# Fused windowed attention and MLP on one core: the early pairs, the weight decoding and the first shared slices put in one written order, with double weight chunks

## The chip, the cores and the metric

One core of a Trainium2 chip runs the whole program. The metric is the device time of one execution in microseconds (us). The kernel before took 674.14 us as the median of three runs (673.58 to 674.37). The engines are TensorE (PE in the profile; PEld is its weight load), VectorE (DVE), ScalarE (ACT), GpSimd (POOL) and SyncE (SP), whose queue issues nearly all DMAs.

## The reference, cut to what matters

```python
# attention: B=4, H=8, S=768, D=64, fp32
scores = scale * q @ k.T                      # per head
keep   = (column < 8) | (0 <= row - column < 96)
scores = where(keep, scores - slope[h] * dist, -1e9)
a = exp(scores - max(scores));  a = a / (sum(a) + 1e-9)
x = (a @ v) laid out as [B*S, H*D] = [3072, 512]
# MLP: w_in [512, 2048], w_out [2048, 512]
h = x @ w_in
g = h * clip(h + 3, 0, 6) / 6
out = g @ w_out                               # [3072, 512]
```

The two weight matrices reach the kernel as 64-bit floats (two 32-bit words for each value) and are turned into 32-bit values on the chip; this is the decoding below. Each 32-bit value is then split in a high and a low part of type fp32r, so that three fp32r products stand for one exact one.

## The kernel before, in words

**Tiling.** The 3072 rows are eight blocks of 384 rows (three tiles of 128). A block's attention is four pairs of heads; 32 pairs in all, numbered n = 0 to 31. The MLP of a block has 16 slices of 128 hidden columns. A slice is a first product (`first`, L165: 12 matmuls of 384 columns into a bank hp), a gate (`gate`: ACT at L182, DVE at L183), a split of the gated values into high and low (`high`: ACT at L191 in the first two blocks, POOL at L189 later; `rest`: DVE at L196) and a second product (`second`, L199: 9 matmuls of 512 columns into three acc banks). TensorE runs `second` of a slice only after `first` of the next slice.

**A pair.** `scores` (matmuls, L818), `weigh` (six DVE sums with a running minimum at L833, six ACT exponentials at L837), `sum_up` (DVE, L847 and L848), `normalize` (six POOL multiplications, L857), `turn` (transposes on TensorE at L865 and L867, copied out to pt at L869), `values` (matmuls, L909) and `put_x` (ACT at L157, DVE at L158).

**The early part** (`banded`, L488). Pairs 0 to 11 (`EARLY` = 12) fill x of the first three blocks. A loop over n scores pair n + 2, normalizes pair n + 1, turns pair n and multiplies pair n - 1 by the values, so four pairs are in work at once. From n = 8 on, halves of the first MLP slices of block 0 are put in between; `FIRST` = 6 such slices run here. After the loop the remaining slices of blocks 0 and 1 alternate ("shared slices": both blocks use the same decoded weights). Blocks 2 to 7 follow, each with the attention of the next block between its slices.

**Decoding** (`decode`, L393). There are 32 chunks of 128x512 values. For one chunk: a DMA (L368); ACT takes the absolute value of the upper word (wz, L376); POOL scales the lower word (we, L380); DVE clamps (L407) and shifts left by three (L408); ACT makes the sign from the upper half word (L387); DVE adds the two (L417); ACT rounds to the high part (w1h or w2h, L421); DVE subtracts for the low part (w1l or w2l, L414). The loads have three buffers (`WORDS`), wz and we two each. `work(pe, dve)` keeps an account of TensorE and DVE time and emits a decoding step when DVE is behind; `decoded_to` forces the steps that a slice needs.

**Order.** TensorE, SP and POOL execute in the order in which the program text emits their instructions (`in_order`, L615, a chain of order-only dependencies). ACT and DVE are ordered by the scheduler from its own estimate of times. `load_next` (L297) issues the load of a later pair behind the matmuls that free its buffer.

Of the kernel before, what the change touches and what calls it, by code (L numbers as in the profile page):

```python
# [9 lines left out]
F32 = mybir.dt.float32  # L10
# [3 lines left out]
I16 = mybir.dt.int16  # L14
F16 = mybir.dt.float16
# [6 lines left out]
P = 128  # L22
NT = 3
# [23 lines left out]
BOTH = 10  # L47
ROOMS = 2
MORE = 3
LEAD = 6  # L50
WAKE = 9
FIRST = 6
WORDS = 3
DOWN = 2.0 ** -95
# [8 lines left out]
class Kernel:  # L63
# [15 lines left out]
    def decoding(self, ctx, loads, bufs, **kw):  # L79

        self.wp = self.pool("wp", loads, ctx=ctx, **kw)
        self.zp = self.pool("zp", bufs, ctx=ctx, **kw)
        self.ep = self.pool("ep", bufs, ctx=ctx, **kw)
# [16 lines left out]
    def constants(self):  # L100
# [4 lines left out]
        self.small = self.const.tile([P, 4], F32, name="small")  # L105
        self.three, self.half = self.small[:, 0:1], self.small[:, 3:4]
        nc.vector.memset(self.three, 3.0)
        nc.vector.memset(self.half, -0.5)
# [8 lines left out]
    def weight_chunk(self, i):  # L117
# [17 lines left out]
        nc.sync.dma_start(out=st, in_=self.w[i])  # L135
# [18 lines left out]
    def put_x(self, x, pair, ps):  # L154
        nc = self.nc
        xh, xl = x
        nc.scalar.copy(out=xh[:, pair, :], in_=ps)  # L157
        nc.vector.tensor_tensor(out=xl[:, pair, :], in0=ps, in1=xh[:, pair, :].bitcast(F32), op=ALU.subtract)  # L158
# [74 lines left out]
    def bank(self, what):  # L233

        s, t, x, o, h = ((self.ps_s, "sp"), (self.ps_t, "tp"), (self.ps_x, "xp"), (self.ps_o, "acc"), (self.ps_h, "hp"))
        pools = {"s": (s, o, o, o), "t": (t, h, h), "x": (x,)}[what] if self.more else {"s": (s, t)[:self.score_banks], "t": (t,), "x": (x,)}[what]
# [129 lines left out]
    def fetch(self, i):  # L366
        self.raw[i] = self.wp.tile([P, 2 * DM], I32, name="wst")
        self.nc.sync.dma_start(out=self.raw[i], in_=self.w[i])  # L368

    def magnitude(self, i):  # L370
# [3 lines left out]
        self.z[i] = self.zp.tile([P, DM], I32, name="wz")  # L374
        self.e[i] = self.ep.tile([P, DM], I32, name="we")
        self.nc.scalar.activation(out=self.z[i].bitcast(F32), in_=words[:, :, 1].bitcast(F32), func=AF.Abs, scale=DOWN)  # L376
        if i == 0:
            self.tc.add_manual_dep(self.nc.cur_bb.bb.instructions[-1], self.held, mybir.DependencyInfo(
                mybir.DependencyClass.NoSync, mybir.DependencyReason.DATA), reason="behind the first pairs")
        self.nc.gpsimd.tensor_scalar(out=self.e[i], in0=words[:, :, 0].bitcast(U32), scalar1=2.0 ** -29, scalar2=0.0, op0=ALU.mult, op1=ALU.add)  # L380

    def signs(self, i):


        top = self.raw[i].bitcast(I16).rearrange("p (c w) -> p c w", w=4)[:, :, 3]
        over = self.e[i].bitcast(F16).rearrange("p (c w) -> p c w", w=2)[:, :, 1]
        self.nc.scalar.activation(out=over, in_=top, func=AF.Sign, scale=-1.0, bias=self.half)  # L387

    def part(self, i, w1, w2):
        f = i // 2  # L390
# [598 lines left out]
```

## Time and profile before

| what | value |
|---|---|
| median of three runs | 674.14 us (673.58 to 674.37) |
| the profiled execution, device time | 675.05 us |
| its span, first to last instruction | 673.2 us |
| busy TensorE, VectorE, ScalarE, GpSimd | 655.6, 406.0, 299.2, 216.1 us |
| mean granted TensorE clock | 0.996 |

The profile is of one execution; what lies around its span is 675.05 - 673.2 = 1.85 us. A busy TensorE is not one at its peak, since ends of matmuls are modelled and matmuls that fill a pause (the kernel's `spin`) count as busy. In rows that list instructions in order of time, the first column is the start and the second the duration; the difference of two starts is what an instruction costs its engine, since the durations of neighbours overlap by about 0.1 us.

### The profile page before, as it was taken

What the parts mean: (1) busy time and instruction counts of PE and PEld (TensorE: products, weight loads), DVE (VectorE), ACT (ScalarE), POOL (GpSimd) and SP (SyncE); (2) the same over time, 40 slices, a digit from 0 to 9 for tenths busy, and PEclk for the clock granted to TensorE, in tenths of its full rate; (3) what the DMA queues carried; (4) which work ended last, traced back from release to release, by engine and by line L of the source; (5) the groups of instructions that cost most, each with busy time, mean ns of one, the idle gap of its engine ahead of it and who ended that gap; (6) DMA issues with size and microseconds to landing.
All of it is one profiled execution on the core that took longest, in us unless ns stands there. A gap on an engine that the chain in (4) does not pass through costs nothing.

```text
span 673.2 us, 11394 instructions
## 1 busy us (share of the span) xinstructions
PE 655.6 (97%) x3963; PEld 586.4 (87%) x3963; DVE 406.0 (60%) x1090; ACT 299.2 (44%) x768; POOL 216.1 (32%) x389
## 2 busy tenths in 40 slices
PE   9888799999999999999999999999999999999996
PEld 7767688889999999899998999899998999989995
DVE  6788789982224776457663777447763677422222
ACT  6899899962225433144332443143331434231111
POOL 5655722210001343234341454314431444302110
PEclk9989999999999999999999999999999999999999
DMA  8678565500003267525644267624555255510001
GB/s 294 180 217 273 174 206 195 188 32 0 1 1 133 69 173 201 153 81 140 178 120 132 87 171 184 173 96 117 141 166 141 78 149 141 142 48 2 0 1 52
DMA packets 60835, 84.72 MB, mean 126 GB/s; under 512 B 8416, under 2 KB 45536, under 8 KB 60768
## 3 DMA queue, kind: packets, MB, share of 16 engines
q1 hardware_dynamic: 60480, 83.64, 42.6%
q8 instruction: 33, 0.54, 0.3%
q14 instruction: 34, 0.28, 0.1%
q10 hardware_dynamic: 288, 0.26, 0.1%
HBM read 62.92 MB, written 20.97 MB: 125 GB/s over the span
## 4 chain that ended last, share of the span: by engine, by line
PE 89%; DMA 3%; DVE 2%; POOL 2%; ACT 2%; issue 1%; SPq 0%; POOLq 0%; DVEq 0%
PE hp L171 38%; PE acc L203 33%; PE xp L909 4%; PE sp L822 2%; DMA wst<-w 2%; PE tp L909 2%; PE sp L203 2%; PE tp L203 2%; PE xp L203 2%; PE tp L822 2%; POOL n L857 1%; PE sp L818 1%; ACT n L837 1%; POOL we L380 1%; ACT we L387 1%
## 5 line engine op out<-in xcount | busy, mean ns | idle before, releaser
L182 ACT ACTIVATE g<-hp,small 128x384 f32<-128x384 f32 x127 | 73.7, 580 | 261.6 <-PE hp L171 234.2
L171 PE MATMUL hp<-xh,w1h 128*128 128x384 f32 x512 | 174.0, 340 | 0.0
L171 PE MATMUL hp<-xh,w1l 128*128 128x384 f32 x512 | 172.7, 337 | 0.0
L171 PE MATMUL hp<-xl,w1h 128*128 128x384 f32 x512 | 171.9, 336 | 0.0
L189 POOL TENSOR_SCALAR gh<-g 128x384 fp32r<-128x384 f32 x96 | 51.8, 540 | 292.7 <-DVE g L183 253.9
L203 PE MATMUL acc<-w2h,gl 128*128 128x512 f32 x336 | 133.1, 396 | 0.0
L203 PE MATMUL acc<-w2l,gh 128*128 128x512 f32 x336 | 132.4, 394 | 0.0
L203 PE MATMUL acc<-w2h,gh 128*128 128x512 f32 x336 | 132.1, 393 | 0.0
L183 DVE SCALAR_TENSOR_TENSOR g<-g,hp 128x384 f32<-128x384 f32 x128 | 69.7, 545 | 101.5 <-ACT g L182 101.3
L857 POOL TENSOR_SCALAR n<-n,sums 128x232 f32<-128x232 f32 (+1 forms) x186 | 101.4, 561 | 36.9 <-DVE sums L848 24.8
L196 DVE TENSOR_TENSOR gl<-g,gh 128x384 fp32r<-128x384 f32 x128 | 79.2, 619 | 53.6 <-POOL gh L189 45.5
L837 ACT ACTIVATE n<-n,least 128x232 f32<-128x232 f32 (+1 forms) x192 | 89.3, 467 | 43.1 <-DVE least L833 42.1
L171 PEld LDWEIGHTS hp<-xh,w1h 128*128 128x128 f32 x512 | 96.3, 188 | 5.5 <-issue 1.5
L171 PEld LDWEIGHTS hp<-xl,w1h 128*128 128x128 f32 x512 | 96.2, 188 | 3.9
L171 PEld LDWEIGHTS hp<-xh,w1l 128*128 128x128 f32 x512 | 96.0, 188 | 0.0
L203 PEld LDWEIGHTS acc<-w2h,gl 128*128 128x128 f32 x336 | 63.0, 188 | 14.7 <-DVE gl L196 1.2
L203 PEld LDWEIGHTS acc<-w2h,gh 128*128 128x128 f32 x336 | 63.3, 188 | 10.3 <-POOL gh L189 0.3
L203 PEld LDWEIGHTS acc<-w2l,gh 128*128 128x128 f32 x336 | 63.2, 188 | 10.3
L882 DVE STREAM_TRANSPOSE blocks<-n 128x256 f32<-128x256 f32 x112 | 43.5, 424 | 29.8 <-POOL n L857 15.2
L793 POOL TENSOR_SCALAR kx<-load 64x504 fp32r<-64x504 f32 (+1 forms) x40 | 31.1, 777 | 63.0 <-PE hp L171 61.4
L833 DVE CUSTOM_DVE_ANT_0 n<-sp,d 128x232 f32<-128x232 f32 (+1 forms) x70 | 23.6, 375 | 29.5 <-PE sp L822 28.9
L380 POOL TENSOR_SCALAR we<-wst 128x512 int32<-128x512 uint32 x32 | 24.0, 751 | 52.0 <-DVE wz L417 24.2
(111 smaller groups left out, 791.1 us busy)
## 6 DMA issues: line engine op xcount, KB each, us to landing
wst<-w SPq DMA_DIRECT2D x32, 512.0 KB, 4.4
load<-pairs SPq DMA_DIRECT2D x22, 636.0 KB, 5.1
there<-blocks SPq DMA_DIRECT2D x52, 256.0 KB, 2.6
load<-pairs SPq DMA_DIRECT2D x32, 384.0 KB, 3.9
weights<-there SPq DMA_DIRECT2D x48, 192.0 KB, 3.8
out<-o SPq DMA_DIRECT2D x23, 256.0 KB, 2.1
weights<-there SPq DMA_DIRECT2D x32, 160.0 KB, 3.2
load<-pairs SPq DMA_DIRECT2D x9, 444.0 KB, 4.0
```

The source lines that it names most:

```text
L171: self.nc.tensor.matmul(hp, lhsT=self.w1(w, f)[:, kt, :], rhs=a[:, kt, :], start=(n == 0), stop=(n == 3 * NKT - 1))
L182: nc.scalar.activation(out=g, in_=hp, func=AF.Relu, bias=self.three, scale=1.0)
L183: nc.vector.scalar_tensor_tensor(out=g, in0=g, scalar=6.0, in1=hp, op0=ALU.min, op1=ALU.mult)
L189: self.nc.gpsimd.tensor_scalar(out=gh, in0=g, scalar1=1.0, scalar2=0.0, op0=ALU.mult, op1=ALU.add)
L196: self.nc.vector.tensor_tensor(out=gl, in0=g, in1=gh.bitcast(F32), op=ALU.subtract)
L203: self.nc.tensor.matmul(acc[tt], lhsT=a[:, tk], rhs=self.w2(w, f), start=(f == 0 and j == 0), stop=(f == NF - 1 and j == 2))
L380: self.nc.gpsimd.tensor_scalar(out=self.e[i], in0=words[:, :, 0].bitcast(U32), scalar1=2.0 ** -29, scalar2=0.0, op0=ALU.mult, op1=ALU.add)
L793: nc.gpsimd.tensor_scalar(out=part["kx"][own, c], in0=k[own, c], scalar1=1.0, scalar2=0.0, op0=ALU.mult, op1=ALU.add)
L837: nc.scalar.activation(out=e[:, j, lo:W], in_=e[:, j, lo:W], func=AF.Exp, bias=self.least[:, i:i + 1], scale=-1.0, accum_out=self.sums[:, ...
L857: nc.gpsimd.tensor_scalar(out=e[:, j, lo:W], in0=e[:, j, lo:W], scalar1=over, scalar2=0.0, op0=ALU.mult, op1=ALU.add)
L882: nc.vector.transpose(out=blocks[:, :, s].rearrange("p b j q -> p j b q"), in_=e[:, :, c:c + P].rearrange("p j (b q) -> p j b q", b=4))
L909: nc.tensor.matmul(xps[j * D:(j + 1) * D, t * P:(t + 1) * P], lhsT=vt[0:K, t, j * D:(j + 1) * D], rhs=self.part(t, j, c, K), start=(c == 0 ...
```

## The change

The early loop's body becomes a function `ahead`. ACT and DVE are also put in the emitted order from the beginning of the early part to the end of the shared slices; TensorE, SP and POOL keep theirs over the whole program. `FIRST` is 2, and the two first slices go into the last three rounds (n = 10 to 12), so slices 2 to 15 of block 0 now all alternate with those of block 1. In the early part the decoding steps are no longer paced by an account but given by a table, `PLAN` (steps in round n); from the first shared slice on, the account paces them.

A chunk holds 128x1024 values, 16 in all, each for two slices. The 32 sign instructions on ACT go; POOL makes the signs of a chunk in one instruction: it multiplies the upper word, read as an integer, by -0.0, in place. DVE joins the shift with an exclusive or of this sign. we has one buffer instead of two, and there are two load buffers of twice the size. The first two weight loads are issued in rounds n = 0 and 1 instead of before the first values.

Pairs 10 and 11 take the form of pairs 0 to 9 (`BOTH` = 12: two heads in one pass over 64 rows each). The load of the next values is emitted before `put_x` instead of after it. The sums get 1e-9 by a tile of constants.

```diff
-BOTH = 10
+BOTH = EARLY
-LEAD = 6
+PLAN = {2: 1, 3: 1, 4: 1, 5: 1, 6: 1, 7: 1, 8: 1, 9: 1, 10: 2, 11: 2, 12: 1}
-FIRST = 6
-WORDS = 3
-DOWN = 2.0 ** -95
+FIRST = 2
+WORDS = 2
+DOWN = 2.0 ** -80
...
     def magnitude(self, i):
         words = self.raw[i].rearrange("p (c w) -> p c w", w=2)
-        self.z[i] = self.zp.tile([P, DM], I32, name="wz")
-        self.e[i] = self.ep.tile([P, DM], I32, name="we")
+        self.z[i] = self.zp.tile([P, 2 * DM], I32, name="wz")
+        self.e[i] = self.ep.tile([P, 2 * DM], I32, name="we")
         self.nc.scalar.activation(out=self.z[i].bitcast(F32), in_=words[:, :, 1].bitcast(F32), func=AF.Abs, scale=DOWN)
...
+        self.nc.gpsimd.tensor_scalar(out=words[:, :, 1].bitcast(F32), in0=words[:, :, 1], scalar1=-0.0, scalar2=1.0, op0=ALU.mult, op1=ALU.mult)
         self.nc.gpsimd.tensor_scalar(out=self.e[i], in0=words[:, :, 0].bitcast(U32), scalar1=2.0 ** -29, scalar2=0.0, op0=ALU.mult, op1=ALU.add)
-    def signs(self, i):
...
-        self.nc.scalar.activation(out=over, in_=top, func=AF.Sign, scale=-1.0, bias=self.half)
...
     def decode(self):
+        self.magnitude(0)
+        yield 0
+        for i in range(N):
+            z = self.z[i]
+            zf = z.bitcast(F32)
+            ts(out=zf, in0=zf, scalar1=LEAST * DOWN, scalar2=MOST * DOWN, op0=ALU.max, op1=ALU.min)
+            yield 1.2
+            stt(out=z, in0=z, scalar=3, in1=self.raw[i].rearrange("p (c w) -> p c w", w=2)[:, :, 1],
+                op0=ALU.logical_shift_left, op1=ALU.bitwise_xor)
+            if i + WORDS < N:
+                self.fetch(i + WORDS)
+            if i + 1 < N:
+                self.magnitude(i + 1)
+            yield 1.8
+            hi, sh = self.part(i, self.w1h, self.w2h)
+            tt(out=z, in0=z, in1=self.e.pop(i), op=ALU.add)
+            nc.scalar.copy(out=hi, in_=sh(zf))
+            yield 1.8
+            self.lower(i)
+            yield 1.8
+        self.decoded_all()
     def work(self, pe, dve):
         self.given[0] += pe
         self.given[1] += dve
-        while self.given[1] < self.given[0] and self.decoded < self.allowed:
+        if self.paced and self.given[1] < self.given[0]:
             self.decode_step()
...
-            self.decoding(words, WORDS, 2, side="right")
+            self.decoding(words, WORDS, (2, 1), side="right")
...
+            self.in_order(start, mybir.EngineType.Activation, mybir.EngineType.DVE)
...
-        self.in_order(start)
+        self.in_order(start, mybir.EngineType.PE, mybir.EngineType.SP, mybir.EngineType.Pool)
...
+    def ahead(self, n, pairs, acc, todo):
+        for pair in {-2: (0, 1), -1: (2, 3)}.get(n, ()):
+            self.distances(pair)
+        if n == EARLY - 2:
+            self.more = False
+            acc.extend(self.acc_tiles())
+        weigh, put = [], None
+        if n + 2 < EARLY:
+            for t in range(NT):
+                weigh.append(pairs[n + 2].scores(t))
+                if n == 0 and t < NT - 1:
+                    self.spin(2)
+            if n < 0:
+                self.spin(5)
+            self.load_next(n + 2, False)
+            if n == -2:
+                self.load(2, True)
+            if n in (0, 1):
+                self.fetch(n)
+        if n >= EARLY - 2:
+            next(todo, None)
+        for t, (score, exps) in enumerate(weigh):
+            score()
+            if t < 2:
+                exps()
+        if n + 1 in (0, 1):
+            for t in range(NT):
+                pairs[n + 1].sum_up(t)
+                pairs[n + 1].normalize(t)
+        elif 2 <= n + 1 < EARLY:
+            pairs[n + 1].sum_up()
+            for t in range(NT):
+                pairs[n + 1].normalize(t)
+        if n > 0:
+            put = pairs[n - 1].values()
+            if put:
+                put[0]()
+        for t in range(NT):
+            if 0 <= n < EARLY:
+                pairs[n].turn(t)
+                if n == 0 and t < NT - 1:
+                    self.spin(3)
+        if weigh:
+            weigh[2][1]()
+        for _ in range(PLAN.get(n, 0)):
+            self.decode_step()
+        if put:
+            put[1]()
+        if n >= EARLY - 2:
+            next(todo, None)
```

More of the change, by code (lines that the diff above doesn't have):

```diff
@@ L104, in constants @@
         make_identity(nc, self.ident)
-        self.small = self.const.tile([P, 4], F32, name="small")
-        self.three, self.half = self.small[:, 0:1], self.small[:, 3:4]
+        self.small = self.const.tile([P, 3], F32, name="small")
+        self.little = self.const.tile([P, 2 * NT], F32, name="little")
+        nc.vector.memset(self.little, 1e-9)
+        self.three = self.small[:, 0:1]
         nc.vector.memset(self.three, 3.0)
-        nc.vector.memset(self.half, -0.5)
     def common(self, xs, banks):
@@ L154, in put_x, with put_high, put_low @@
     def put_x(self, x, pair, ps):
[L155 to L158, printed above, removed]
+        self.put_high(x, pair, ps)
+        self.put_low(x, pair, ps)
+    def put_high(self, x, pair, ps):
+        self.nc.scalar.copy(out=x[0][:, pair, :], in_=ps)
+    def put_low(self, x, pair, ps):
+        self.nc.vector.tensor_tensor(out=x[1][:, pair, :], in0=ps, in1=x[0][:, pair, :].bitcast(F32), op=ALU.subtract)
     def split_q(self, h, qd, q1, q2):
@@ L366, in fetch @@
     def fetch(self, i):
-        self.raw[i] = self.wp.tile([P, 2 * DM], I32, name="wst")
+        self.raw[i] = self.wp.tile([P, 4 * DM], I32, name="wst")
         self.nc.sync.dma_start(out=self.raw[i], in_=self.w[i])
@@ L393, in decode, with lower @@
+        if i % 2 == 0:
+            return w1[half][:, :, f * P:(f + 2) * P], lambda a: a.rearrange("p (k c) -> p k c", k=NKT)
+        return w2[half][:, f:f + 2, :], lambda a: a.rearrange("p (s c) -> p s c", s=2)
+    def lower(self, i):
+        hi, sh = self.part(i, self.w1h, self.w2h)
+        lo, _ = self.part(i, self.w1l, self.w2l)
+        self.nc.vector.tensor_tensor(out=lo, in0=sh(self.z.pop(i).bitcast(F32)), in1=hi.bitcast(F32), op=ALU.subtract)
+        self.decoded = i + 1
     def decode(self):
@@ L397, in decode @@
         nc = self.nc
[L398 to L399 removed]
+        ts, stt, tt = nc.vector.tensor_scalar, nc.vector.scalar_tensor_tensor, nc.vector.tensor_tensor
+        N = NF
         self.magnitude(0)
[L401 to L422 removed]
@@ new lines, in decode @@
+        yield 0
[11 more added lines that the diff above has]
+            yield 1.8
+            hi, sh = self.part(i, self.w1h, self.w2h)
+            tt(out=z, in0=z, in1=self.e.pop(i), op=ALU.add)
[3 more added lines that the diff above has]
+            yield 1.8
@@ L579, in banded @@
+                    self.ahead(n, pairs, acc, todo)
                 for _ in todo:
@@ L658, in general_setup @@
         self.weights()
[L659 removed]
+        self.decoding(self.ctx, 1, (1, 1))
         self.ap_ = self.pool("ap", 1)
```

151 lines of the change are left out of this document (38 added, 113 removed).

## The prediction, made before the changed kernel was built or run

> **What bounds the kernel now.** I read the engines' shares first, then a table by stretches of time, cut where the values matmuls of some pairs begin, then the instructions of single engines in order of time. The table's columns are length, then busy time and count of PE, PEld, DVE, ACT and POOL, granted clock, DMA share, GB/s.
>
> ```profile
> PE 655.6 (97%) x3963; PEld 586.4 (87%) x3963; DVE 406.0 (60%) x1090; ACT 299.2 (44%) x768; POOL 216.1 (32%) x389
> ...
> 0.00:18.69 18.69, 17.71 (x122) 14.77 (x122) 12.07 (x71) 12.45 (x45) 10.60 (x35) 1.00 0.78 267
> 18.69:22.77 4.08, 4.08 (x43) 3.21 (x42) 3.40 (x17) 3.88 (x15) 2.37 (x6) 1.00 0.78 204
> 22.77:27.34 4.57, 4.08 (x43) 3.21 (x42) 3.40 (x17) 4.05 (x15) 2.47 (x6) 1.00 0.74 198
> 27.34:57.01 29.67, 24.95 (x238) 20.80 (x239) 24.79 (x100) 28.78 (x91) 20.14 (x38) 0.94 0.75 234
> 57.01:94.60 37.59, 31.81 (x240) 26.46 (x239) 32.10 (x75) 32.91 (x76) 18.38 (x26) 1.00 0.64 207
> 94.60:106.29 11.69, 11.21 (x58) 9.97 (x57) 11.02 (x23) 10.90 (x19) 2.88 (x4) 1.00 0.59 196
> 106.29:673.20 566.91, 561.79 (x3225) 508.01 (x3225) 319.20 (x796) 206.19 (x510) 159.23 (x278) 1.00 0.38 108
> ```
>
> TensorE is the engine of the whole, but not of the first 94.6 us. There ACT is the fullest (28.78 of 29.67 us). The rows of TensorE below show the values of pairs 0, 2, 7 and 11 (those of pair 1 begin at 22.77), the next first product, the last wait, and two pieces of the later chain.
>
> ```profile
> 18.69 1.32 PE L909 MATMUL xp<-pt,load 128*64 128x128 f32 x20
> 27.34 1.32 PE L909 MATMUL xp<-pt,load 128*64 128x128 f32 x20 [0.49 <-DVE xl L158]
> 57.01 1.54 PE L909 MATMUL xp<-pt,load 128*64 128x128 f32 x24
> 93.35 1.32 PE L909 MATMUL xp<-pt,load 128*64 128x128 f32 x20
> 94.60 0.45 PE L171 MATMUL hp<-xh,w1h 128*128 128x384 f32 x1
> 106.29 0.51 PE L203 MATMUL sp<-w2h,gl 128*128 128x512 f32 x1 [0.48 <-DVE gl L196]
> ...
> 146.28 2.10 PE hp L171 x12
> 148.39 2.08 PE acc L203 x9
> ```
>
> One first product costs 2.10 us, one second product 2.08. After 106.29 the chain holds TensorE work back to back, so anything gained must come before, as the time at which pair 11's values end (94.60 now), less the MLP work that is no longer done by then.
>
> **The break-even.** At 94.60 the kernel before has done five first and four second products of block 0 (slice 5 begins right at 94.60, the second product of slice 4 behind it). The changed order has done two and one. The missing three of each are 3 x (2.10 + 2.08) = 12.5 us of TensorE time to be made up; the wait of 0.48 us at 106.29 is the only loss I count behind. So pair 11's values must end before 94.60 + 0.48 - 12.5 = **82.6 us**; each us earlier is a us won.
>
> **The change part by part.** *What a round costs now.* With no decoding in it, a round costs 4.08 us when it scores one of pairs 0 to 3 (a smaller first tile, as with pairs 8 to 11) and 4.57 us with a full pair. From pair 2 to pair 7 five rounds take 29.67 us, 5.93 each: the 1.36 us more is decoding on a full ACT. What a chunk costs there:
>
> ```profile
> L387 ACT ACTIVATE we<-wst,small 128x512 f16<-128x512 int16 x5 | 4.4, 876 | 0.0
> L376 ACT ACTIVATE wz<-wst 128x512 f32<-128x512 f32 x6 | 4.0, 685 | 0.0
> L421 ACT CAST w2h<-wz 128x512 fp32r<-128x512 f32 x2 | 1.3, 626 | 0.0
> L837 ACT ACTIVATE n<-n,least 128x232 f32<-128x232 f32 x42 | 20.2, 483 | 1.1 <-DVE least L833 0.6 <-POOL n L857 0.5
> L837 ACT ACTIVATE n<-n,least 128x128 f32<-128x128 f32 x9 | 3.6, 402 | 0.8 <-DVE least L833 0.8
> L158 DVE TENSOR_TENSOR xl<-xp,xh 128x384 fp32r<-128x384 f32 x7 | 3.9, 552 | 0.0
> L414 DVE TENSOR_TENSOR w1l<-wz,w1h 128x512 fp32r<-128x512 f32 x2 | 1.4, 688 | 0.0
> L407 DVE TENSOR_SCALAR wz<-wz 128x512 f32<-128x512 f32 x6 | 3.0, 497 | 0.4 <-ACT wz L376 0.3
> L380 POOL TENSOR_SCALAR we<-wst 128x512 int32<-128x512 uint32 x6 | 5.0, 831 | 0.5
> L857 POOL TENSOR_SCALAR n<-n,sums 128x232 f32<-128x232 f32 x43 | 21.5, 518 | 8.7 <-DVE sums L848 5.9 <-PE hp L867 2.1 <-DVE least L833 0.6
> L869 ACT COPY pt<-tp 128x512 f32<-128x512 f32 x5 | 2.9, 573 | 0.0
> ```
>
> On ACT the two exponentials give (483 - 402)/104 = 0.78 ns for each further column, so a double chunk costs 685 + 400 and 626 + 400 ns: 2.1 us, against 2 x (0.876 + 0.685 + 0.626) = 4.4 for two chunks. On DVE (688 - 552)/128 = 1.06 ns a column: 1.23 us for the lower part at 1024 columns. No row shows the joined shift and exclusive or; it lies between 0.69 (one such instruction at half the width) and 2 x 0.69; as a two-input operation it is nearest to the lower part, so 1.23, and the sum as much. The clamp is between 0.50 and 1.0, I take 0.8. Together 4.5 us in four steps. On POOL the scaling lies between 0.83 and 1.66; I take 1.3, and the same for the new sign instruction, which is of the same kind: 2.6 us.
>
> *Rounds 1 to 9.* The table gives one step to each of rounds 2 to 9. On ACT a step is 2.1/4 = 0.53 us on average. ACT stays the fullest (DVE 3.40 + 4.5/4 = 4.5; TensorE 4.1 to 4.3). So 4.57 + 0.53 = 5.1 us for rounds 2 to 5; 4.9 for 6 and 7, which score small pairs but turn full ones; 4.08 + 0.53 = 4.6 for 8 and 9. With 4.08 for round 1: 4.08 + 20.4 + 9.8 + 9.2 = 43.5 us. If the steps hide behind waits altogether, it is 39.2; if a round costs as now, 4.08 + 8 x 5.93 = 51.5.
>
> *An added wait.* we has one buffer, so POOL's scaling of chunk 1 (emitted in round 4) waits for DVE's sum of chunk 0 (round 5), and pair 6's six multiplications stand behind it on POOL. The sum ends some 4.3 us into round 5 (DVE's 3.40 less the 0.55 of `put_x` behind it, 1.23, and 0.2 of handing over), the scaling at 5.6; six multiplications at 0.518 take to 8.7. TensorE would turn pair 6 after scores and values of round 6, some 2.8 us into it, so from 5.1 + 2.8 - 1.0 = 6.9 to 7.9 if the values start as early as they can: **0.8 us**, with 0 and 3.1 (all six) as ends. At chunk 2 (round 8) the first products of round 10 cover it.
>
> *Start.* The first values stay at 18.69; two weight instructions of ACT that stood ahead of the first copies there could give back up to 1.1 us. The later weight loads leave the first loads of the pairs more room (267 GB/s there now); I count nothing.
>
> *Rounds 10 to 12.* Values of pair 9 begin at 18.69 + 43.5 + 0.8 = 63.0, plus 1.0 of the first product placed ahead of them, since a round of 5.1 leaves about 1 us of TensorE idle for its 2.1 (ends 0 and 2.1). Then values 9 (1.25, from 93.35 to 94.60), turn 10 (ten transposes, 1.1), first and second (2.10, 2.08), values 10 and turn 11 (2.35), the last copy on ACT that values 11 wait for (0.57 and 0.2 of handing over) and values 11 (1.25): 10.9 us.
>
> ```profile
> 28.76 0.27 PE L867 MATMUL hp<-ident,n 128*128 128x128 f32 x1
> 28.87 0.27 PE L865 MATMUL hp<-ident,n 128*128 128x128 f32 x1
> ```
>
> These two starts give the 0.11 us of a transpose. Pair 11's values end at 64.0 + 10.9 = **74.9 us**, 7.7 us before the break-even.
>
> *The shared slices.* Here DVE and ACT have no longer the scheduler's freedom. Following the account through the code, every second slice has the sum of a chunk between its gate and its `rest`, and the rounding on ACT ahead of its `high`. An undisturbed chain from gate to low part looks like this:
>
> ```profile
> 148.43 0.58 ACT L182 ACTIVATE g<-hp,small 128x384 f32<-128x384 f32 x1 [1.67 <-PE hp L171]
> 149.04 0.56 DVE L183 SCALAR_TENSOR_TENSOR g<-g,hp 128x384 f32<-128x384 f32 x1 [1.56 <-ACT g L182]
> 149.63 0.51 ACT L191 CAST gh<-g 128x384 fp32r<-128x384 f32 x1 [0.62 <-DVE g L183]
> 150.17 0.56 DVE L196 TENSOR_TENSOR gl<-g,gh 128x384 fp32r<-128x384 f32 x1 [0.58 <-ACT gh L191]
> ...
> L203 PEld LDWEIGHTS acc<-w2h,gl 128*128 128x128 f32 x336 | 63.0, 188 | 14.7 <-DVE gl L196 1.2
> ```
>
> It takes 2.3 us. The sum (1.25) and the rounding (0.95 between starts) between its second and third piece make it 4.5. TensorE needs the low part after one second and one first product and two matmuls (2.08/9 = 0.23 each): 2.08 + 2.10 + 0.46, less 0.19 for loading it: 4.45. So the margin is about nothing. I take 0.15 us of waiting for every two slices; 26 slices, in which the remaining 13 chunks are made, give **2.0 us**. Otherwise the stretch is easier than now: for two slices (8.4 us) DVE has 2 x 0.94 + 4.5 = 6.4 us, where it is busy 11.02 of 11.69 before.
>
> What could break the margin is POOL:
>
> ```profile
> 48.11 1.14 DVE L417 CUSTOM_DVE_ANT_0 wz<-wz,we 128x1024 uint16<-128x1024 uint16 x1
> ...
> 93.02 0.69 DVE L417 CUSTOM_DVE_ANT_0 wz<-wz,we 128x1024 uint16<-128x1024 uint16 x1
> ...
> 47.99 0.71 POOL L380 TENSOR_SCALAR we<-wst 128x512 int32<-128x512 uint32 x1
> ```
>
> A sum, elsewhere 0.69 us, took 1.14 beside a POOL instruction that had begun 0.12 earlier: it ended about as if it had begun with POOL's end. POOL's instructions now last some 1.3 us. POOL's scaling comes right after the sum and ends before `rest`; the next sign instruction comes when its load lands, after `rest` by my count. The low end of the unknown is no wait; the high end is 1.3 us for every two slices. The Trainium skill ("SBUF — State Buffer", section "Who interferes with whom") says that a DVE instruction with two SBUF inputs and a GpSimd instruction that reads SBUF exclude each other for the whole instruction. By that the rows above are a full block and the high end is what a badly timed sign instruction costs; the trace agrees, 0.45 us for what was left of 0.71.
>
> The other edits come to nothing: pairs 10 and 11 in the narrower form save TensorE time under ACT's; the sums' other form is one DVE instruction for another; a load emitted before `put_x` waits for the same matmuls on SP as before.
>
> **The sum.** 82.6 - 74.9 - 2.0 = 5.7 us against the profiled execution's 675.05 (673.2 of span and 1.85 around it, which I leave): 669.4. It was 0.9 above the median of the runs shown, so **668.5 us**.
>
> **Rivals.** *A: the steps hide, rounds run at the pace of 18.69 to 27.34.* 4.3 us off the rounds, the 0.8 and 1.1 of the start go too: 668.5 - 6.2 = 662. For it: the pace is shown, and DVE and ACT wait for each other there. Against: ACT is 4.05 of 4.57 full in such a round. *B: the fixed order costs the rounds what the scheduler saved*, since one late instruction now holds all behind it. At 5.93 a round 8.0 us are added: 676.5; at 5.5, 673. For it: five engines hand a pair on within each round. Against: TensorE and POOL had this order already, and ACT is relieved. *C: slower, by the shared slices.* A POOL sign instruction meets `rest` in every second slice; from 7.7/13 = 0.6 us a time the gain is gone; at 0.8 the time is 668.5 + 13 x 0.65 = 677. For it: the margin of nothing and the row of 1.14. Against: a load of 512 KB takes 4.4 us to land here, and the double one should bring its signs after `rest`. That the change doesn't do what it says I hold for excluded by the code: signs and order move as described.
>
> ```profile
> wst<-w SPq DMA_DIRECT2D x32, 512.0 KB, 4.4
> ```
>
> **How the numbers follow.** Likeliest as worked out 0.45 (its own range 664.5 to 672, all faster); A 0.20 (faster); B 0.17 (0.02 faster, 0.07 the same, 0.08 slower); C 0.18 (0.04 the same, 0.14 slower). A run of this kernel tells a change from none at about 0.2%, 1.35 us. Faster 0.45 + 0.20 + 0.02 = 0.67, same 0.11, slower 0.22. The range goes from A's 662 less 1, so 661, to 677, where C lies; a part of A below and of B and C above is left out.
>
> **What would show it.** In the profile after: values of pair 11 ending near 75 us (82.6 if nothing is won, 70 for A); rounds 2 to 5 near 5.1 us by the starts of the values; no sign instruction on ACT and POOL sign instructions of about 1.3 us; a POOL wait for DVE's sum in round 5; small waits of TensorE for gl in every second shared slice. I am wrong if rounds are longer than 5.9 us, or if these waits are above 0.6 us each.

## The result and the profile after

The changed kernel takes **664.07 us** (median; 663.72 to 664.76), the kernel before beside it 674.25 us (673.58 to 675.03): a ratio of 0.985, 95% interval 0.9833 to 0.9867. That is 10.2 us less, where 5.7 were forecast: right in direction, inside the range, but nearer to rival A (662) than to the forecast (668.5). The profiled execution took 664.76 us with a span of 662.9.

The engines' shares of the page after:

```profile
PE 652.2 (98%) x3963; PEld 582.1 (88%) x3963; DVE 402.6 (61%) x1028; ACT 271.8 (41%) x702; POOL 231.5 (35%) x389
```

The work went as described: 66 instructions fewer on ACT and 62 fewer on DVE, and 15.4 us more on POOL. TensorE's matmuls are the same 3963. Its idle time fell from 17.6 to 10.7 us and its busy time by 3.4, so most of the gain is time in which it waited, and it is found by place. The table by stretches of the kernel after, cut at the starts of the values of pairs 0 to 9, then at the end of pair 11's values (71.60) and the first product of block 2 (198.40); columns as in the tables of before:

```profile
17.47:21.33 3.86, 3.86 (x44) 3.22 (x42) 3.21 (x17) 3.86 (x16) 2.60 (x7) 1.00 1.13 336
21.33:25.20 3.87, 3.87 (x45) 3.23 (x43) 3.43 (x17) 3.87 (x16) 2.22 (x6) 1.00 0.85 353
25.20:30.31 5.11, 3.94 (x45) 3.26 (x43) 5.08 (x18) 5.11 (x17) 4.23 (x7) 1.00 0.94 334
30.31:35.20 4.89, 4.15 (x44) 3.47 (x45) 4.65 (x18) 4.89 (x18) 4.46 (x9) 1.00 0.53 167
35.20:40.20 5.00, 4.21 (x49) 3.54 (x49) 4.80 (x18) 5.00 (x17) 2.64 (x5) 1.00 0.86 307
40.20:45.78 5.58, 5.21 (x48) 3.43 (x49) 4.38 (x18) 4.85 (x16) 5.49 (x10) 1.00 0.69 218
45.78:50.24 4.46, 4.21 (x48) 3.53 (x49) 3.72 (x18) 4.08 (x16) 3.87 (x9) 1.00 0.76 233
50.24:55.12 4.88, 3.99 (x46) 3.31 (x47) 4.36 (x18) 4.60 (x18) 3.42 (x7) 1.00 0.74 218
55.12:60.31 5.19, 4.84 (x42) 4.19 (x42) 4.34 (x17) 5.19 (x17) 2.92 (x4) 1.00 0.72 284
60.31:71.60 11.29, 11.09 (x103) 8.95 (x102) 7.01 (x12) 6.71 (x14) 6.69 (x13) 1.00 0.25 71
71.60:198.40 126.80, 126.80 (x632) 112.00 (x631) 88.35 (x118) 60.36 (x91) 36.14 (x28) 1.00 0.28 100
198.40:662.90 464.50, 459.52 (x2715) 415.98 (x2713) 258.71 (x685) 152.37 (x418) 148.38 (x263) 1.00 0.43 119
```

The same cuts of the kernel before, whose pair 11 ended at 94.60 and whose block 2 began at 209.00:

```profile
94.60:209.00 114.40, 113.92 (x570) 102.28 (x569) 69.96 (x133) 64.75 (x114) 13.75 (x19) 1.00 0.22 72
209.00:673.20 464.20, 459.08 (x2715) 415.71 (x2713) 260.26 (x685) 152.33 (x416) 148.35 (x263) 1.00 0.43 119
```

The last row of both is the same (464.50 and 464.20), so all that was won was won before block 2: 10.6 us. Of the 32 slices of blocks 0 and 1, 27 were left at the end of pair 11's values before and 30 are left after. At the prediction's 4.18 us for both products of a slice these are 112.9 and 125.4 us, so the kernel before lost 1.5 us behind 94.60 and the kernel after loses 1.4 behind 71.60. Pair 11 ended 23.0 us earlier, three slices cost 12.5 of it, and 0.1 came from the waits: 10.6. By place, 1.2 us come from the start, 5.5 from the seven rounds between the values of pairs 0 and 7 (38.32 us before, 32.77 after), and 3.7 from there to the end of pair 11's values (37.59 less the 12.5 of the slices before, 21.36 after).

What a round waits for, in a row of TensorE after:

```profile
40.20 1.54 PE L917 MATMUL xp<-pt,load 128*64 128x128 f32 x24 [0.78 <-ACT n L848]
```

What releases the values is ACT, in the rows of all rounds from 30.31 to 55.12 (0.26 to 1.17 us). The added wait of the prediction stands in the rows of POOL:

```profile
36.25 1.18 POOL L385 TENSOR_SCALAR wst<-wst 128x1024 f32<-128x1024 int32 x1
39.79 1.19 POOL L386 TENSOR_SCALAR we<-wst 128x1024 int32<-128x1024 uint32 x1 [2.36 <-DVE wz L422]
41.07 6.21 POOL L865 TENSOR_SCALAR n<-n,sums 128x232 f32<-128x232 f32 x12
```

The scaling of chunk 1 stands 2.36 us for DVE's sum of chunk 0, and the multiplications of a pair come behind it, as forecast. The next stretch, 40.20 to 45.78, is the longest of the rounds.

A shared slice with a sum and a rounding in it, in order of time:

```profile
85.24 1.22 DVE L414 SCALAR_TENSOR_TENSOR wz<-wz,wst 128x1024 int32<-128x1024 int32 x1
...
85.86 1.57 POOL L385 TENSOR_SCALAR wst<-wst 128x1024 f32<-128x1024 int32 x1 [4.15 <-ACT wz L384]
...
87.28 0.55 DVE L191 SCALAR_TENSOR_TENSOR g<-g,hp 128x384 f32<-128x384 f32 x1 [0.82 <-ACT g L190]
...
87.75 1.22 DVE L422 CUSTOM_DVE_ANT_0 wz<-wz,we 128x2048 uint16<-128x2048 uint16 x1
...
89.00 1.05 ACT L423 CAST w1h<-wz 128x1024 fp32r<-128x1024 f32 x1 [1.75 <-DVE wz L422]
...
89.95 0.51 ACT L199 CAST gh<-g 128x384 fp32r<-128x384 f32 x1
...
90.49 0.56 DVE L204 TENSOR_TENSOR gl<-g,gh 128x384 fp32r<-128x384 f32 x1 [1.53 <-ACT gh L199]
...
91.11 0.50 PE L211 MATMUL sp<-w2h,gl 128*128 128x512 f32 x1
```

Gate (87.28), sum, rounding, high part, low part (90.49) follow each other as the prediction laid them out. In the view of waits, TensorE's loading of these weights waited 13 times, 0.3 us at the longest:

```profile
PEld sp L211 <- DVE gl L204: 3.7, 13, 0.3
```

The starts of the first products stand 4.28 and 4.19 us apart in turn, so the chain costs about 0.1 us in every second slice.

### The profile page after: what moved, and what is told of

It reads as the page before. It is cut to its first block, busy times and chain, and to the rows that moved or that the text cites. A ratio compares the mean times of both kernels' runs of the same rounds, so it can differ in the third digit from the quotient of the medians.

```text
span 662.9 us, 11223 instructions
## 1 busy us (share of the span) xinstructions
PE 652.2 (98%) x3963; PEld 582.1 (88%) x3963; DVE 402.6 (61%) x1028; ACT 271.8 (41%) x702; POOL 231.5 (35%) x389
## 4 chain that ended last, share of the span: by engine, by line
PE 92%; ACT 4%; DMA 2%; issue 1%; DVE 0%; POOL 0%; SPq 0%; POOLq 0%; ACTq 0%
PE hp L179 40%; PE acc L211 34%; PE xp L917 3%; ACT n L848 2%; PE sp L827 2%; PE sp L211 2%; PE tp L917 2%; PE tp L211 2%; PE xp L211 2%; PE tp L827 2%; PE xp L371 1%; DMA there<-blocks 1%; ACT pt L877 1%; PE sp L823 1%; DMA weights<-there 1%
## 5 line engine op out<-in xcount | busy, mean ns | idle before, releaser
L204 DVE TENSOR_TENSOR gl<-g,gh 128x384 fp32r<-128x384 f32 x128 | 77.9, 609 | 67.4 <-POOL gh L197 45.3
L865 POOL TENSOR_SCALAR n<-n,sums 128x232 f32<-128x232 f32 (+1 forms) x186 | 99.2, 549 | 28.2 <-DVE sums L856 13.5
L211 PEld LDWEIGHTS acc<-w2h,gh 128*128 128x128 f32 x336 | 63.3, 188 | 10.6 <-POOL gh L197 0.6
L211 PEld LDWEIGHTS acc<-w2l,gh 128*128 128x128 f32 x336 | 63.2, 188 | 10.2
L890 DVE STREAM_TRANSPOSE blocks<-n 128x256 f32<-128x256 f32 x112 | 43.5, 424 | 31.4 <-POOL n L865 18.6
L385 POOL TENSOR_SCALAR wst<-wst 128x1024 f32<-128x1024 int32 x16 | 23.7, 1480 | 54.6 <-ACT wz L384 54.5
L798 POOL TENSOR_SCALAR kx<-load 64x504 fp32r<-64x504 f32 (+1 forms) x40 | 31.1, 777 | 19.2 <-PE hp L179 17.6
```

The costliest lines, as they stand in the source:

```text
L204: self.nc.vector.tensor_tensor(out=gl, in0=g, in1=gh.bitcast(F32), op=ALU.subtract)
L211: self.nc.tensor.matmul(acc[tt], lhsT=a[:, tk], rhs=self.w2(w, f), start=(f == 0 and j == 0), stop=(f == NF - 1 and j == 2))
L798: nc.gpsimd.tensor_scalar(out=part["kx"][own, c], in0=k[own, c], scalar1=1.0, scalar2=0.0, op0=ALU.mult, op1=ALU.add)
L865: nc.gpsimd.tensor_scalar(out=e[:, j, lo:W], in0=e[:, j, lo:W], scalar1=over, scalar2=0.0, op0=ALU.mult, op1=ALU.add)
L890: nc.vector.transpose(out=blocks[:, :, s].rearrange("p b j q -> p j b q"), in_=e[:, :, c:c + P].rearrange("p j (b q) -> p j b q", b=4))
```

## The experiments

Experiments 1 to 7 and 11 alter the changed kernel, 8 to 10 the kernel before; 12 repeats the changed one. The ratios are all to the kernel before.

**1. The order of ACT and DVE given back to the scheduler.**

```diff
-            self.in_order(start, mybir.EngineType.Activation, mybir.EngineType.DVE)
```

> The changed kernel with ACT and DVE ordered by the scheduler again in the early part and the shared slices; TensorE, SP and POOL keep the emitted order, all else is as in the change. Theory (the gain is ACT relieved in the early rounds plus slices put off; the written order of ACT and DVE is worth little by itself): 664 to 667 us, values of pair 11 ending at 71 to 74 us. Rival (the written order is what gained): 669 to 674 us, rounds near the 5.9 us of before.

Measured: 702.36 us, ratio 1.0398 (1.0382 to 1.0414), so the written order is worth 38 us here. Pair 11's values begin at 84.2 instead of 70.3. The shared slices, up to 166 us, are mostly 5.1 to 7.6 us apart instead of 4.2. The table by stretches shows DVE full at 101 to 130 us:

```profile
101.00:130.00 29.00, 23.41 (x95) 19.65 (x95) 29.00 (x28) 15.03 (x20) 13.97 (x10) 0.86 0.50 176
```

Its DVE rows in order of time, with POOL's beside them:

```profile
101.44 1.35 POOL L385 TENSOR_SCALAR wst<-wst 128x1024 f32<-128x1024 int32 x1 [3.49 <-ACT wz L384]
101.69 1.64 DVE L412 TENSOR_SCALAR wz<-wz 128x1024 f32<-128x1024 f32 x1
...
103.71 1.71 DVE L414 SCALAR_TENSOR_TENSOR wz<-wz,wst 128x1024 int32<-128x1024 int32 x1
```

Two things fill DVE. The scheduler draws the decoding forward: the ten slices that begin from 103.84 to 159.60 hold ten sums, one in every slice, where the changed kernel has one in two. With the pieces of the gate (0.55 and 0.56) such a slice needs 0.68 + 1.22 + 1.22 + 1.21 + 1.1 = 5.4 us of DVE, estimated from the undisturbed rows, against 4.18 of TensorE. And clamp and exclusive or fall to where POOL's instructions run, and take 1.64 and 1.71 us there instead of 0.68 and 1.22. Both theories had the loss far too small: neither counted either of the two.

**2. The signs on ACT again, at the double size.** POOL's instruction goes; DVE shifts alone; ACT's `Sign` over 128x1024 comes back.

```diff
-        self.nc.gpsimd.tensor_scalar(out=words[:, :, 1].bitcast(F32), in0=words[:, :, 1], scalar1=-0.0, scalar2=1.0, ...)
...
-            stt(out=z, in0=z, scalar=3, in1=..., op0=ALU.logical_shift_left, op1=ALU.bitwise_xor)
+            ts(out=z, in0=z, scalar1=3, scalar2=None, op0=ALU.logical_shift_left)
...
+            nc.scalar.activation(out=over, in_=top, func=AF.Sign, scale=-1.0, bias=self.half)
```

> The changed kernel with the signs made by ACT again, one instruction for a double chunk (about 1.5 us by the 0.88 us at half the width), the shift an instruction of its own on DVE, POOL only scaling. Theory (ACT sets the early rounds): three signs fall into rounds 2 to 12, 4.5 us, so about 668 us (666.5 to 670), values of pair 11 ending near 75 to 76. Rival (order and put-off slices are all): 664 us within 1. Rival (the signs are most of the gain): 672 us or more.

Measured: 669.81 us, ratio 0.9921 (0.9904 to 0.9938). About half of the gain is lost, and most of that not where ACT is the fullest engine. From the first values to the end of pair 11's it takes 55.3 us, against 54.1 after. That is a balance: the two rounds with a sign of 1.47 us in them take 6.17 and 6.52 instead of 5.00 and 5.58, and the two rounds before them, where POOL's first sign is gone, 4.45 and 4.31 instead of 5.11 and 4.89. The stretch from there to block 2 takes 131.9 against 126.8. In order of time, its ACT and DVE in a shared slice (gate on ACT: L194, `high`: L203):

```profile
104.60 1.49 ACT L420 ACTIVATE we<-wst,small 128x1024 f16<-128x1024 int16 x1
...
105.93 1.10 ACT L388 ACTIVATE wz<-wst 128x1024 f32<-128x1024 f32 x1
106.92 0.59 ACT L194 ACTIVATE g<-hp,small 128x384 f32<-128x384 f32 x1
...
110.22 0.51 ACT L203 CAST gh<-g 128x384 fp32r<-128x384 f32 x1
```

The sign makes ACT reach the gate late, and the chain that had a margin of nothing starts late: TensorE waits for gh in 12 slices. In the written order an engine that is half empty (77.02 us busy of 131.90) still costs time, because the work stands ahead of the gate.

**3. POOL's scaling behind DVE's sum.** The scaling of the next chunk is emitted after the sum that frees its buffer, so nothing on POOL stands behind a wait.

```diff
 # the scaling, moved out of magnitude() into scaling(i), is called behind the sum
             tt(out=z, in0=z, in1=self.e.pop(i), op=ALU.add)
             nc.scalar.copy(out=hi, in_=sh(zf))
+            if i + 1 < N:
+                self.scaling(i + 1)
```

> The changed kernel with POOL's scaling of the next chunk emitted after DVE's sum of the present one instead of before it, so that the multiplications of a pair no longer stand behind a waiting POOL instruction. Theory (the wait in round 5 delays the turn of pair 6, 5.58 us for that round against about 4.6): 0.8 to 1.1 us faster, 663.1 us. Rival (other engines fill the time, the round is as long anyway): 664.1 us.

Measured: 664.18 us, ratio 0.9835 (0.9822 to 0.9848). The table by stretches has the round that took 5.58 after:

```profile
40.21:45.21 5.00, 4.21 (x49) 3.54 (x49) 4.91 (x18) 4.67 (x16) 4.48 (x7) 1.00 0.72 241
```

The wait cost 0.58 us, and pair 11's values begin 0.75 us earlier (69.51), 0.14 of it from the start. The 0.8 to 1.1 us of the theory were a little too much, and in the time of the whole it can't be told from the changed kernel.

**4. The decoding step behind the gate's last pieces.** In the shared slices `high` and `rest` come ahead of the decoding step, so the step no longer stretches the chain.

```diff
-            self.work(2.1, 0.47)
             yield
             ...
             gl = self.rest(g, gh)
-            self.work(0, 0.47)
+            self.work(2.1, 0.94)
```

> The changed kernel with the decoding step of a shared slice emitted after the high and low part of its gated values instead of between gate and high part. Theory (the 0.12 us wait of TensorE for the low part, 13 times, goes): 1.3 to 1.6 us faster, 662.6 us. Rival (the wait moves to the other of two slices or to the gate): 664.1 us.

Measured: 674.36 us, ratio 0.9996 (0.9987 to 1.0005): the whole gain is lost. The early part is as after (pair 11's values at 69.38). The slices stand 4.33 and 5.07 us apart. In order of time:

```profile
118.26 1.22 DVE L422 CUSTOM_DVE_ANT_0 wz<-wz,we 128x2048 uint16<-128x2048 uint16 x1
...
119.51 1.05 ACT L423 CAST w2h<-wz 128x1024 fp32r<-128x1024 f32 x1 [1.76 <-DVE wz L422]
...
120.60 1.23 DVE L397 TENSOR_TENSOR w2l<-wz,w2h 128x1024 fp32r<-128x1024 f32 x1 [1.12 <-ACT w2h L423]
121.74 0.55 DVE L191 SCALAR_TENSOR_TENSOR g<-g,hp 128x384 f32<-128x384 f32 x1
...
123.97 1.12 POOL L385 TENSOR_SCALAR wst<-wst 128x1024 f32<-128x1024 int32 x1 [3.27 <-ACT wz L384]
124.12 2.04 DVE L414 SCALAR_TENSOR_TENSOR wz<-wz,wst 128x1024 int32<-128x1024 int32 x1
```

Two things changed at once, and the theory had counted neither. Sum, rounding and lower part now follow each other on DVE and ACT ahead of the next gate (121.74), since the code lets no gate piece in between. And the exclusive or now begins 0.15 us behind a POOL sign and takes 2.04 us instead of 1.22: rival C's block, 0.82 us. The wait of TensorE falls on the slice with the first, whose sum begins late by the second; how much belongs to each was not separated.

**5. The first two weight loads ahead of the first values again.** Only the two `fetch` calls move.

```diff
-            if n in (0, 1):
-                self.fetch(n)
...
                 self.load(2, False)
+                self.fetch(0)
+                self.fetch(1)
```

> The changed kernel with the first two weight loads (1 MB each) issued where they were before, ahead of the first values. Theory (the first values came 1.2 us earlier because two weight instructions of ACT left the place ahead of them): values of pair 0 stay near 17.4 us, total within 0.7 us of the changed kernel, 664.1 us. Rival (the loads were what held them): values of pair 0 at 18.5 to 20 us, 665.3 us or more.

Measured: 665.68 us, ratio 0.9857 (0.9834 to 0.9879). The first values begin at 18.62, against 16.6 to 17.5 in the profiles of the kernels that keep the late loads and the written order; all that follows is shifted and otherwise the same. The row of TensorE that was late:

```profile
17.41 0.35 PE L823 MATMUL sp<-load 64*128 64x128 f32 x1 [1.44 <-DMA load<-pairs]
```

The pair's own load came late behind the weights'. These two loads are twice as large as the two that stood there in the kernel before. This is what the rival said (18.5 to 20 us, 665.3 us or more). The intervals of the times overlap with those of the changed kernel, so this rests on the trace.

**6. Six first slices again.** `FIRST` back to 6 in the changed kernel, paced by the account while they run.

```diff
-FIRST = 2
+FIRST = 6
...
+                self.paced = True
                 for _ in todo:
                     pass
```

> The changed kernel with six first slices of block 0 instead of two: four slices of block 0 alone after pair 11, before the shared ones, with the decoding paced there too. Theory (a double chunk feeds four slices when both blocks share it and two when block 0 is alone; three double chunks are some 13.5 us of DVE, with four gates 17.3 us, against 16.7 us of TensorE, and their chains show): 3 to 8 us slower than the changed kernel, about 669 us. Rival (the number of first slices does not matter once the order is written): 664 us within 1.

Measured: 693.35 us, ratio 1.0267 (1.0245 to 1.0288). The four further slices, with pair 11's values among them and nothing of block 1 between them, take 45.8 us:

```profile
72.90:118.70 45.80, 27.61 (x104) 21.68 (x105) 22.02 (x22) 11.25 (x15) 8.21 (x7) 0.72 0.24 84
```

No engine is full, and the granted clock is 0.72. Its view of waits has the reason:

```profile
PEld acc L211 <- ACT w2h L423: 14.8, 2, 7.8
```

A slice now needs a chunk's parts as soon as they can be made, and TensorE stands through all steps of a chunk, one behind the other. The expectation had this more than 20 us too cheap.

**7. The steps in fewer rounds.** Rounds 2 to 5 are left without decoding, and rounds 6 to 9 take two steps each.

```diff
-PLAN = {2: 1, 3: 1, 4: 1, 5: 1, 6: 1, 7: 1, 8: 1, 9: 1, 10: 2, 11: 2, 12: 1}
+PLAN = {6: 2, 7: 2, 8: 2, 9: 2, 10: 2, 11: 2, 12: 1}
```

> The changed kernel with no decoding step in rounds 2 to 5 and two steps in each of rounds 6 to 9, the same 13 steps in all. Theory (a step costs the round what it costs its engines): rounds 3 to 5 fall from 5.0 to about 4.4 us and rounds 6 to 9 rise by as much, total within 1 us of the changed kernel. Rival (the steps lie in pauses and the rounds are set by the hand-over from engine to engine): rounds 3 to 5 stay near 5.0 us; then two steps in a round cost more than they save and the total is 1 to 3 us longer.

Measured: 667.19 us, ratio 0.9881 (0.9864 to 0.9899). The table by the starts of the values:

```profile
28.44:32.52 4.08, 4.08 (x46) 3.45 (x44) 3.43 (x17) 4.08 (x16) 2.84 (x8) 1.00 0.70 219
32.52:36.66 4.14, 4.14 (x50) 3.50 (x48) 3.43 (x17) 4.14 (x17) 2.69 (x7) 1.00 0.72 209
36.66:43.60 6.94, 4.21 (x51) 3.54 (x49) 3.83 (x18) 5.64 (x20) 4.65 (x9) 0.94 0.72 203
43.60:52.12 8.52, 7.01 (x49) 6.01 (x49) 5.48 (x19) 5.74 (x17) 4.20 (x9) 0.65 0.30 92
```

A round of a full pair without a step takes 4.08 to 4.14 us. The same rounds with one step take 4.89 and 5.00 after: a step costs such a round 0.8 to 0.9 us. The round before them takes 3.86 here and 5.11 after, 1.25 more, but there parts of two steps run in it. With two steps rounds took up to 8.52; there the clock fell as well, so what the second step costs by itself isn't separated. The theory was right about the rounds without steps, the rival about the total, some 3 us longer than the changed kernel.

**8. Two first slices alone, in the kernel before.**

```diff
-FIRST = 6
+FIRST = 2
```

> The kernel before with two first slices of block 0 in the early part instead of six; nothing else is changed. Theory (what counts is that ACT and DVE have fewer chunks to decode before pair 11's values): rounds to pair 7 as before (57 us), then pair 11 ending near 80 us, and 2 to 4 us faster than before, about 671.5 us. Rival (put-off slices are worth nothing without the written order): within 1 us of before, or slower.

Measured: 683.12 us, ratio 1.012 (1.0096 to 1.0145). Up to pair 7 the starts are those of before (57.11 against 57.01). Then three slices are gone from the time before pair 11's values end (two first products and one second instead of five and four), 12.5 us of TensorE, but pair 11's values begin only 6.2 us earlier (87.2 against 93.35). That is 4.9 us behind the break-even of 83.6 worked out below. By the end of pair 11's values this kernel has the lower parts of 10 of its 32 chunks (13 before), where the changed one has decoded two of its 16: fewer slices leave most of the early decoding where it was.

**9. A written order alone, in the kernel before.** ACT and DVE also follow the emitted order up to the end of the shared slices.

```diff
-        self.in_order(start)
+        self.in_order(start, mybir.EngineType.PE, mybir.EngineType.SP, mybir.EngineType.Pool)
...
             for _ in self.halves(todo):
                 pass
+            self.in_order(start, mybir.EngineType.Activation, mybir.EngineType.DVE)
```

> The kernel before with ACT and DVE also held to the emitted order in the early part and the shared slices; slices, chunks and signs are as before. Theory after the run with the scheduler's order (38 us lost: the order belongs to the emission that was made for it): the emission of before was not made for it, so no gain, 674 to 684 us. Rival (the written order is a gain of its own): 664 to 670 us, rounds near 5 us.

Measured: 707.39 us, ratio 1.048 (1.0456 to 1.0505). Rounds go up to 14.3 us and pair 11's values begin at 107.5. The order in which the old text emits its work is a bad one to execute: it is rival B, and far worse than its price; no gain was expected, but 23 us less of a loss.

**10. Two first slices and the decoding put off, in the kernel before.** The scheduler stays, but the account allows only as many steps early as four chunks need.

```diff
-FIRST = 6
+FIRST = 2
...
-            self.allowed = 3 * NF + 2
+            self.allowed = 3 * 4 + 2
```

> The kernel before with two first slices and with its early decoding ended after the four chunks that these need; the rest of the 32 chunks is decoded in the shared slices. Single chunks, signs on ACT, and the scheduler's order of ACT and DVE stay. With two first slices alone 11 of 32 chunks were made before pair 11's values ended (88.5 us), in the changed kernel 4. Theory (the early part is as long as the decoding in it): pair 11 ending at 74 to 80 us, 665 to 671 us in all if the scheduler leaves the shared slices alone. Rival (without the written order and the double chunks the put-off decoding costs the shared slices what the early part wins): pair 11 ending by 80 us as well, but 674 us or more.

Measured: 676.23 us, ratio 1.0027 (1.0014 to 1.0041). Pair 11's values end at 82.7, 0.9 us ahead of the break-even, and the way from there to block 2 takes 128.2 us, 2.8 more than the 125.4 of its slices. By 82.7 seven chunks have their lower parts, not four, as the scheduler draws some forward; the changed kernel has two double ones, as much as four. Rows of its table by stretches, and one of TensorE in the first of them:

```profile
68.00:71.00 3.00, 1.43 (x11) 0.96 (x10) 1.55 (x7) 2.13 (x7) 0.05 (x1) 1.00 0.41 121
...
77.00:81.00 4.00, 3.88 (x28) 2.98 (x28) 2.36 (x4) 2.11 (x5) 0.00 (x0) 0.50 0.15 23
...
69.52 0.41 PE L865 MATMUL tp<-ident,n 128*128 128x128 f32 x2 [0.77 <-ACT pt L869]
```

From the values of pair 7 on, the rounds still take 9.6, 5.7, 5.9 and 3.6 us; the first of them holds a first and a second product (4.2 us). TensorE pauses (1.43 of 3.00 us busy), and then runs at a granted clock of 0.50. Four of its pauses in the last rounds, 2.6 us together, are like the row above: transposes into the one bank tp wait until ACT has copied the ones before out of it. In the kernel before the same wait stands in the view of waits for 57.01 to 94.60:

```profile
PE tp L865 <- ACT pt L869: 3.6, 4, 1.8
```

The changed kernel has none of it there: its last rounds turn pairs in two banks, tp and sp, by turns, an edit that the experiments 8 to 10 do not have and that no run tries alone. So slices and less decoding do not make the gain without the rest, but how much of the missing rest is the second bank stays open.

**11. The rounding behind the high part.** The late scaling of experiment 3, and in the shared slices ACT's rounding is emitted with the lower part, behind `high` and `rest`; the sum stays where it is.

```diff
             tt(out=z, in0=z, in1=self.e.pop(i), op=ALU.add)
-            nc.scalar.copy(out=hi, in_=sh(zf))
+            behind = self.paced
+            if not behind:
+                nc.scalar.copy(out=hi, in_=sh(zf))
             ...
             yield 1.8
+            if behind:
+                nc.scalar.copy(out=hi, in_=sh(zf))
             self.lower(i)
```

> The changed kernel with two moves in the written order: POOL's scaling of the next chunk after DVE's sum (as in the run where only that was moved), and, in the shared slices, ACT's rounding of a chunk emitted behind the high part of the gated values, with the step of the lower part. Theory (0.7 us of early time; and the low part of a slice no longer waits for the rounding, so TensorE's wait of 0.09 us at every second slice goes, 1.2 us): 1.5 to 2 us faster than the changed kernel beside it, 662.3 us. Rival (the lower part, now behind the rounding, delays the next gate as it did when the high part was put first): slower by some us.

Measured: **661.63 us**, ratio 0.98 (0.9785 to 0.9815), below both kernels and 2.8 us below the changed one beside it (experiment 12). Its stretch from the end of pair 11's values to block 2:

```profile
70.20:195.10 124.90, 124.90 (x632) 113.54 (x631) 91.13 (x118) 61.77 (x91) 38.79 (x28) 1.00 0.30 102
```

It is 1.9 us shorter than the 126.80 after, 0.15 for each of the 13 chunks made there, and its first products stand 4.13 and 4.19 us apart. No wait for gl is left. Experiment 3 has the late scaling too and kept the 4.28, so the rounding out of the chain is what made the difference, and the chain that the prediction priced is what TensorE waited for.

**12. The changed kernel again.**

> The changed kernel once more, to stand beside the next run on the same chip: 664.1 us.

Measured: 664.46 us, ratio 0.9843 (0.9827 to 0.9859); pair 11's values begin at 69.78, 0.5 earlier than in the first profile, as do the first values.

## Why the prediction was right in sign and 4.5 us short

**The break-even held in form.** The three missing slices and the end of pair 11's values decide, and what lies behind block 2's start is the same. Its size was 1.0 us off: the prediction counted one wait of 0.48 behind 94.60, and the small ones together were 1.5. At the prediction's prices the break-even lies at 83.6, not 82.6. The forecast of 74.9 for the end of pair 11's values was 3.3 us too late; 71.60 lies nearer to the 70 that stood for rival A.

**Start: mis-sized by 1.2 us, and put down to the wrong thing.** "I count nothing" stood for the loads' room; the first values came at 17.47 instead of 18.69. With the weight loads ahead again they came at 18.62 (experiment 5), and the row waits for the pair's own load. The loads are not the whole of it: with late loads but the scheduler's order (experiment 1) the values began at 18.39, and with early loads but the written order in the kernel before (experiment 9) at 17.81. Order and loads both count; how much of the 1.2 each gives isn't separated, as the loads of experiment 5 are twice those of before, and the first values of the changed kernel itself come at 17.47 in one run and 16.99 in another.

**Rounds: 2.5 us too long in sum, the terms further off.** From 17.47 to 60.31 they took 42.8 us; the prediction had 43.5, 0.8 for the wait and 1.0 for the first product, 45.3. About 5.1 us for a round with a step was measured as 4.89 to 5.11. But it was written as 4.57 + 0.53, and experiment 7 has it as 4.1 + 0.9. The undisturbed round of 4.57 before takes 3.87 after, with ACT busy through all of it, and full rounds later 4.08 to 4.14. So it was not ACT's work that made it 4.57; that it was the scheduler's order is argued, not shown. What rival A said (that the pace of before's first rounds is reached and the steps hide) is half true: the pace is better than that and the steps don't hide. Round 2 was the clearest miss, 3.87 instead of 5.1. Its step holds no DVE work, and its ACT part ran only behind the next values, in round 3:

```profile
25.54 1.17 ACT L384 ACTIVATE wz<-wst 128x1024 f32<-128x1024 f32 x1
```

The 5.93 us of a round before was not all decoding either: the granted clock was 0.50 from 40.28 to 43.68 us, behind a pause of TensorE of 2.36 us. That is the 0.94 in the prediction's own table, and up to 1.7 us (an estimate, half of the 3.40) of the 29.67 that it put down to a full ACT. After, the clock stays at 1.00 in all rounds.

**The tail owes something to an edit that has no term.** The forecast of 10.9 us (11.3 measured) counts no wait of a transpose for its bank. In the kernel before such waits for ACT's copy come to 3.6 us from 57.01 on; the changed one has a second bank there, which the prediction does not name. That the tail came out is so in part luck; how large a part is not shown.

**"ACT stays the fullest" is true of the rows and not enough as a bound.** ACT is busy through whole rounds (5.11 of 5.11, 5.00 of 5.00), and a sign of 1.47 us put into a round (experiment 2) lengthened it by 1.17 and 0.94 us. But the two rounds before them, where POOL's first sign was gone, were 0.66 and 0.58 us shorter with ACT just as full (4.45 of 4.45, 4.31 of 4.31), so that part grew by 1.2 us in all, not 2.9. In a written order the place of an instruction counts beside the engine's load.

**The prices of the double chunk were good.** Rows of groups by shape, 14 to 72 us of the kernel after:

```profile
L384 ACT ACTIVATE wz<-wst 128x1024 f32<-128x1024 f32 x4 | 4.7, 1165 | 0.0
...
L422 DVE CUSTOM_DVE_ANT_0 wz<-wz,we 128x2048 uint16<-128x2048 uint16 x3 | 3.7, 1219 | 0.1
L385 POOL TENSOR_SCALAR wst<-wst 128x1024 f32<-128x1024 int32 x3 | 3.5, 1179 | 0.7 <-ACT wz L384 0.7
```

ACT takes 1.17 and about 1.05 (forecast 2.1 for both), the sum 1.22 (1.23), POOL's sign 1.18 (1.3). The added wait was forecast at 0.8 us and is 0.58 by the round that experiment 3 shortens.

**Shared slices: 2.0 us forecast, 1.4 measured** at the prices of the prediction, and 1.9 against the same stretch without the wait (experiment 11). The chain of 4.5 against a margin of 4.45 was the most exact step, and it named what could still be had.

**Rival C's mechanism is there and did not strike.** The block of a DVE instruction by POOL's sign is seen in experiments 1 and 4 (2.04 us for 1.22). In the changed kernel DVE's exclusive or begins first (85.24) and POOL's sign behind it (85.86), so it is POOL that takes 1.57 instead of 1.18, and nobody waits for it. The sign did come after `rest`, but not for the prediction's reason, a load that lands late: the load of its chunk was issued at 78.46 and takes 4.8 us to land, and the row has the sign wait for ACT's absolute value of the same words (84.64 to 85.79). So the place was right and the reason wrong; that the exclusive or would then run beside it was not seen. **Rival B** is what the old emission gives (experiment 9), not this one.

**The sum.** Start 1.2, round 2 1.2, round 1 and the other rounds with the first product and the wait 1.2, the tail -0.4, the break-even 1.0 and the shared waits 0.6 make, before rounding, 4.9 us more than the 5.7 forecast: the 10.6 of block 2's start. All but the tail erred to one side, towards too small a gain, and so rival A's number was nearer although the steps do not hide.

**No one part makes the gain.** In the kernel before, two first slices alone cost 1.2%, the order alone 4.8%, and the slices with put-off decoding 0.3%. In the changed one, without the order it is 4.0% slower than before, with six first slices 2.7% slower, and with ACT's signs about half of the gain goes. Double chunks alone and the second bank for the transposes alone were not tried, so the order, the slices and the signs are shown to be needed here, and what the other two give stays open.

## What to carry to other kernels

Where engines execute in a written order, cost each instruction by what stands behind it on its engine, not by its engine's load: a rounding of 1.05 us ahead of a short piece that TensorE needs cost 0.15 us in every second slice on an engine half empty, and putting it behind that piece gave 1.9 us. List every edit of a change with a term of its own, even one of a single bank. A written order is part of the emission it was written for; it was worth 38 us with this one and cost 32 us with the old one. Compare two orders by a break-even on the engine that bounds the rest (the time at which a stage ends, less the work still to be done), and check every small wait behind it.

## What the runs showed of the hardware

A DVE instruction beside a POOL one can cost nearly the sum of both, and who began first decides who pays: the exclusive or took 2.04 us when it began 0.15 us behind a POOL sign of 1.12, and 1.22 when it began first, with POOL's sign then at 1.57. A clamp, which reads one tensor, took 1.64 instead of 0.68 in the same neighbourhood. The Trainium skill ("SBUF — State Buffer", section "Who interferes with whom") says that the instruction issued first holds the shared ports for its whole length and that issue order decides who blocks. The rows agree about who pays, and nearly about how much: 2.04 is 1.22 and 0.82 of the 0.97 us that were left of POOL's, and 1.57 is 1.18 and 0.39 of the 0.60 that were left of the exclusive or.

The granted clock of TensorE fell to 0.50 behind sparse stretches: from 72 to 82 us of experiment 10, after 1.43 us of work in the 3.00 from 68 on, where no row shows a pause above 0.80 us. I had not counted on losing clock by pauses that short. Elsewhere the pauses ahead of it were longer: 2.36 us in the kernel before, 2.73 in experiment 7 (0.65 in one round), up to 7.5 in experiment 6 (0.72 over 45.8 us).
